# Smaller TensorE tiles for the query repeats and the key sums, another order of the first loads, and a new plan, in a fused sketched-attention and feed-forward kernel

## The chip, the cores and the metric

The kernel runs on one core of a Trainium2 chip. The metric is the device time of one execution in microseconds (us): the median of three runs. A profile of one further execution says how the time is spent. The engines are named as the profile names them: PE is TensorE's matmuls and PEld its weight loads, DVE is VectorE, ACT is ScalarE, POOL is GpSimd, and SP is the engine that mostly issues DMAs. A "q" behind an engine's name (SPq, ACTq) is its instruction queue, where DMAs are issued.

## The reference

Four batches of four heads, 1088 tokens each, 32 numbers a head. Queries and keys are sketched: two products with 8x32 matrices, then the outer product of the two, 64 features. Attention is then a sum over keys, with no softmax; its output goes through a feed-forward layer with a squared relu.

```python
def phi(x):                                   # 64 features of a token
    a = np.einsum('rd,bhsd->bhsr', S1, x)
    b = np.einsum('rd,bhsd->bhsr', S2, x)
    return np.einsum('bhsi,bhsj->bhsij', a, b).reshape(*x.shape[:-1], r * r)
q_p, k_p = (phi(q), phi(k))
kv = np.einsum('bhsf,bhsd->bhfd', k_p, v)     # key sums
z = np.sum(k_p, axis=2)
num = np.einsum('bhsf,bhfd->bhsd', q_p, kv)   # read-out
den = np.einsum('bhsf,bhf->bhs', q_p, z)[..., None] + 1e-06
attn = (num / den).astype(np.float32)
x = attn.transpose(0, 2, 1, 3).reshape(4352, 128)
r = np.maximum(x @ w_in, 0.0)                 # 128 -> 2048
out = ((r * r) @ w_out).astype(np.float32)    # 2048 -> 128
```

Attention is computed in float32, the feed-forward layer in bfloat16.

## The kernel before

**The plan.** The kernel is written as a graph of operations. Each has a cost on one or more engines, operations that it depends on, buffers that it takes, and a priority worked out from a due time. Ahead of the launch a list scheduler (`Graph.run`) walks through the graph with these costs and sorts the operations by their planned start. Each engine then executes its own instructions strictly in that order, and real waits come from semaphores. So an operation that is planned early but is late on the chip holds back what is queued behind it on its engine.

**Buffers.** PSUM holds three h buffers of two banks (128 x 1024 float32), one o buffer (the feed-forward output) and one a buffer. Tensors of a batch (kin, kT, qin, qT, vin, vp, ka, kp, kvz, qp) exist twice, by batch parity.

**Attention of a batch**, by the lines of the profile:
- Loads of k, q and v on SP's queue (L297, L333, and L340 for the last 64 tokens of v, which go to a tile of their own, vtl). For batch 0, k and q come in two parts, and the first values go on ScalarE's queue.
- VectorE transposes keys in 32x32 blocks (L365). Key sketches (L379): per chunk of 32 tokens a column tile of 32, 128 rows, S1 and S2 side by side. ScalarE copies the S1 half (L387), VectorE multiplies both into kp, 64 features a head (L395).
- Values are copied into vp beside a column of ones (L350, L353), on GpSimd, or for batch 0 on ScalarE.
- Key sums (L412): for each of nine steps of 128 tokens and each head, weights are 64 features of kp, and the 33 columns of vp are moved; heads go alternately to the two 64-column halves. The sum is copied to the state kvz in two copies (L425), each head's 64 features on the partition half where its sketch of the query will be, the rest zero.
- VectorE transposes queries (L434). Query repeats (L447): S1 repeated along one index of the 64 features and S2 along the other, by one product each. A product takes a pair of heads (64 rows of qT) and gives 128 rows, two heads of 64 features; the two pairs stand in two banks of an h buffer. There are three groups of up to 384 columns, and an h buffer each for S1 and S2.
- ScalarE copies the S1 buffer (L456), VectorE multiplies (L460) into qp.
- Read-out (L477): per chunk of 32 tokens a column tile of 32, weights qp, moved the state of a head pair, 66 columns. VectorE divides (L487 to L489), TensorE transposes (L500), and ScalarE or VectorE copies to xT (L506), the feed-forward input.

**Feed-forward** works in nine blocks of tokens (384, seven times 512, 384) and eight steps of 256 hidden units: two products (L527) into an h buffer, relu on ScalarE (L536), square on VectorE (L543), two accumulating products into o (L550). A block ends with a transpose by VectorE (L557) and four or eight stores (L566).

**The weights** come through six loads on GpSimd's queue (L275, L279), behind a one-column copy that reads the last key column (`gate`, L271), so that they start when batch 0's keys are there.

In numbers of the trace, a float32 product stands as two records of weights and two of matmul (two passes).

Of the kernel before, what the change touches and what calls it, by code (L numbers as in the profile page):

```python
# [15 lines left out]
SEM = 0.07  # L16
LOOK = 0.12
DMA_FIRST = 1.05
DMA_LAST = 1.2
# [9 lines left out]
class Op:  # L29
    def __init__(self, name, alts, fn, deps, pri, alloc, uses, port, dma, after):  # L30
        self.name, self.alts, self.fn, self.pri = name, alts, fn, pri
        self.deps = [d for d in deps if d is not None]
        self.alloc, self.uses, self.port, self.dma = alloc, uses, port, dma
        self.after = [d for d in after if d is not None]
        self.look = LOOK
        self.start = self.end = self.eng = None


class Graph:

    def __init__(self, slots):
        self.ops = []
        self.slots = {k: [[0.0, None] for _ in range(n)] for k, n in slots.items()}

    def add(self, name, alts, fn, deps=(), pri=0.0, alloc=(), uses=(), port=(), dma=None, after=()):
        op = Op(name, alts, fn, deps, pri, list(alloc), list(alloc) + list(uses), port, dma, after)
        for b in op.uses:
            b.pending += 1
        self.ops.append(op)
        return op  # L50

    def slot_time(self, buf):
        best = None
        for kind in buf.kinds:
            for i, (t, b) in enumerate(self.slots[kind]):
                if b is not None and b.pending:
                    continue
                if best is None or t < best[0] - 0.3:
                    best = (t, (kind, i))
        return best  # L60

    def run(self):
        eng_free, port_free, pipe = {}, 0.0, 0.0
# [8 lines left out]
        while ready:  # L72
            cands = []
            for o in ready:
                t_slot = 0.0
                ok = True
                for b in o.alloc:
                    s = self.slot_time(b)
                    if s is None:
                        ok = False  # L80
                        break
                    t_slot = max(t_slot, s[0] + SEM)
                if not ok:
                    continue
                best = None
                for e, (busy, lat, *pen) in o.alts.items():
                    pen = pen[0] if pen else 0.0
                    t = max(eng_free.get(e, 0.0), t_slot)
                    for d in o.deps:
                        t = max(t, d.end + (SEM if d.eng != e else 0.0))  # L90
                    for d in o.after:
                        t = max(t, d.start)
                    if e in o.port:
                        t = max(t, port_free)
                    if o.dma is not None and e != "POOL" and len(lanes) >= 8:
                        t = max(t, lanes[-8])
                    if best is None or t + lat + pen < best[0]:
                        best = (t + lat + pen, t, e, busy, lat)
                cands.append((best[1], o, best))
            assert cands, "no operation can start: " + ", ".join(o.name for o in ready[:20])  # L100
            t0 = min(c[0] for c in cands)
            _, o, (_, t, e, busy, lat) = min(
                (c for c in cands if c[0] <= t0 + c[1].look), key=lambda c: (c[1].pri, c[0]))
            for b in o.alloc:
                b.slot = self.slot_time(b)[1]
                self.slots[b.slot[0]][b.slot[1]] = [t, b]
            o.start, o.end, o.eng = t, t + lat, e
# [5 lines left out]
            eng_free[e] = t + busy  # L113
            if e in o.port:
# [16 lines left out]
def act(n):  # L131
    return (0.833e-3 * n + 0.17, 0.833e-3 * n + 0.2)


def dve(n, rate=1.042e-3, fix=0.07):
    return (rate * n + fix, rate * n + fix + 0.04)


def pool(n, rate=2.4e-3):
    return (rate * n + 0.12, rate * n + 0.16)  # L140


def pe(t):
    return (t, t + 0.2)


@with_exitstack
def kernel(
    ctx: ExitStack,
    tc: tile.TileContext,  # L150
    q: bass.AP,
    k: bass.AP,
    v: bass.AP,
    S1: bass.AP,
    S2: bass.AP,
    moe_w_in: bass.AP,
    moe_w_out: bass.AP,
    out: bass.AP,
):
    nc = tc.nc  # L160
    B, H, S, D = q.shape
    R = S1.shape[0]
    F = R * R
    d_ff = moe_w_in.shape[1]
# [5 lines left out]
    assert (B, H, D, R, S) == (4, 4, 32, 8, 1088)  # L170

    sb = ctx.enter_context(tc.tile_pool(name="sb", bufs=1))
    ps = ctx.enter_context(tc.tile_pool(name="ps", bufs=1, space=bass.MemoryType.PSUM))

    def T(name, shape, dt=F32):
        return sb.tile(shape, dt, name=name, tag=name)

    def P(name, shape, dt=F32):
        return ps.tile(shape, dt, name=name, tag=name)

    NH, NA, NR, NB = 3, 1, 4, 2
    G = Graph({"h": NH, "o": 1, "a": NA, "r": NR, "g": NR, "osb": 3, "den": 3, "A": 2})
# [8 lines left out]
        "A": [T(f"A{i}", [128, 2, 384]) for i in range(2)],  # L191
# [7 lines left out]
    ident = T("ident", [128, 128], BF16)  # L199
    S_sb = T("S_sb", [128, 32])  # L200
    ST = T("ST", [128, 32])
    mk4 = T("mk4", [128, H])
    mk2 = T("mk2", [128, 2])
    SK = T("SK", [128, 2, H, R])
    SR = T("SR", [128, 2, 2, R, R])
# [8 lines left out]
    vtl = [T(f"vtl{i}", [32, H, 2, D]) for i in range(NB)]  # L214
# [3 lines left out]
    kvz = [T(f"kvz{i}", [128, 2, 2, D + 1]) for i in range(NB)]  # L218
# [5 lines left out]
    for x, src in ((0, S1), (1, S2)):  # L224
        def f(e, x=x, src=src):
            en = nc.sync if e == "SP" else nc.scalar
            en.dma_start(out=S_sb[x::2, :], in_=src[None, :, :].to_broadcast([8, R, D]))  # L227
        SU[x] = add(f"S{x}", {"SP" if x else "ACT": (0.4, 2.0)}, f, pri=-200, dma=0.05)
    o_mkz = add("mkz", {"DVE": dve(4)}, lambda e: nc.vector.memset(mk4, 0.0), pri=-100)

    def f_mk(e):
        for h in range(H):
            nc.vector.memset(mk4[32 * h : 32 * h + 32, h : h + 1], 1.0)
        nc.vector.tensor_tensor(out=mk2, in0=mk4[:, 0:2], in1=mk4[:, 2:4], op=ALU.add)
    o_mk = add("mk", {"DVE": (0.4, 0.45)}, f_mk, [o_mkz], pri=-100)
    o_ST = add("ST", {"DVE": dve(32)}, lambda e: nc.vector.transpose(ST, S_sb), SU, -98)
    STx = ST[:, 0 : 2 * R].rearrange("p (r x) -> p x r", x=2)

    o_SR = []
    for x in range(2):  # L240
        def f(e, x=x):
            s = STx[:, x]
            s = s[:, None, None, :] if x else s[:, None, :, None]
            nc.vector.tensor_tensor(
                out=SR[:, x], in0=s.to_broadcast([128, 2, R, R]),
                in1=mk2[:, :, None, None].to_broadcast([128, 2, R, R]), op=ALU.mult)
        o_SR.append(add(f"SR{x}", {"DVE": dve(128)}, f, [o_ST, o_mk], -96))

    def f_SK(e):
        nc.vector.tensor_tensor(  # L250
            out=SK, in0=STx[:, :, None, :].to_broadcast([128, 2, H, R]),
            in1=mk4[:, None, :, None].to_broadcast([128, 2, H, R]), op=ALU.mult)
    o_SK = add("SK", {"DVE": dve(64)}, f_SK, [o_ST, o_mk], -97)

    z_ops = {}
    for i in range(NB):
# [4 lines left out]
        z_ops[i] = add(f"z{i}", {"POOL": (0.6, 0.7)}, f_z, pri=-100 + i)  # L261
# [3 lines left out]
        ident, iot, 0, op=ALU.is_equal), [o_iota], -60)  # L265

    wo_src = moe_w_out.rearrange("(G c e) d -> c G (e d)", c=128, e=E)
    wo_dst = w_out.rearrange("c (G e) d -> c G (e d)", e=E)
    o_win, o_wout = [], []
    gate = T("gate", [128, 1])  # L270
    o_gate = add("gate", {"POOL": (0.1, 0.15)}, lambda e: nc.gpsimd.tensor_copy(gate, kin[0][:, S - 1 : S]), [], -45)  # L271
    gated = [o_gate]
    for lo, hi in ((0, 1), (1, 2), (2, 4)):
        def f(e, lo=lo, hi=hi):
            nc.gpsimd.dma_start(out=w_in[:, 512 * lo : 512 * hi], in_=moe_w_in[:, 512 * lo : 512 * hi])  # L275
        o_win.append(add(f"w_in{lo}", {"POOL": (0.9, 3.0)}, f, [z_ops[1]] + gated, -40 + lo, dma=0.8 * (hi - lo)))
# [3 lines left out]
        o_wout.append(add(f"w_out{lo}", {"POOL": (1.0, 3.0)}, f, [z_ops[1]] + gated, -39.5 + lo, dma=0.9 * (hi - lo)))  # L280
# [10 lines left out]
    def attention(b, vt):  # L291
        i = b % NB
        mine = lambda key, op: hist.setdefault((b, key), []).append(op)

# [7 lines left out]
        def tok(j, g):  # L302
            if j == 8:
# [326 lines left out]
```

## Time and profile before

| | us |
|---|---|
| median of 3 runs (132.34, 134.12, 134.55) | 134.12 |
| span of the profiled execution (first to last instruction) | 130.5 |
| PE busy | 115.0 |
| DVE busy | 96.6 |
| ACT busy | 81.6 |
| POOL busy | 11.1 |
| mean granted clock of TensorE | 0.979 of full |

The profiled execution's span lies inside its time; what lies around it is the difference to the runs, 3.6 us against the median. Busy times of engines overlap, and a PE that is busy is not PE at its peak, since the ends of its pipelined matmuls are modelled. The page cuts the span into 40 slices of 3.26 us and gives each engine's busy share of a slice in tenths. The chain of waits follows the last instruction back, each time to what released it, so its pieces add up to the span.

### The profile page before, as it was taken

How to read it: one execution, taken by the hardware profiler on the slowest of the kernel's cores; microseconds unless marked ns; L12 is line 12 of the kernel's file. 1: busy time of each engine (PE TensorE's matmuls, PEld its weight loads, DVE VectorE, ACT ScalarE, POOL GpSimd, SP SyncE). 2: the span in 40 equal slices, each digit the busy share in tenths (PEclk: the TensorE clock that was granted, in tenths of full speed). 3: DMA queues.
4: the chain of work that ended last, by engine and by line, in shares of the span. 5: the costliest groups of instructions: out<-in, count | busy, mean ns of one | idle time of the engine just before them, and what ended most of it. 6: DMA issues, size and time to landing. Idle time of an engine off the chain costs nothing.

```text
span 130.5 us, 3742 instructions
## 1 busy us (share of the span) xinstructions
PE 115.0 (88%) x1572; PEld 62.2 (48%) x1572; DVE 96.6 (74%) x170; ACT 81.6 (63%) x108; POOL 11.1 (9%) x30
## 2 busy tenths in 40 slices
PE   0279599599999899999999999999999999999930
PEld 0256365353565455455445655556355544444500
DVE  2486367969969999969837888798268977878840
ACT  0065023377636749986525979885377699999910
POOL 4091000504250000000000000000000000000000
PEclk9999959999999999999999999999999999999996
DMA  1999999996700210220130001301300040031402
GB/s 21 296 135 242 328 254 260 254 225 223 159 3 0 51 17 0 40 45 0 28 58 0 5 0 28 57 0 25 60 0 5 0 80 5 3 65 18 78 16 50
DMA packets 24225, 10.22 MB, mean 78 GB/s; under 512 B 19472, under 2 KB 22928, under 8 KB 24208
## 3 DMA queue, kind: packets, MB, share of 16 engines
q1 hardware_dynamic: 22280, 8.57, 28.1%
q0 software_dynamic: 992, 1.05, 5.3%
q10 hardware_dynamic: 936, 0.37, 1.3%
q8 instruction: 12, 0.20, 0.6%
q14 instruction: 5, 0.04, 0.1%
HBM read 8.80 MB, written 2.23 MB: 85 GB/s over the span
## 4 chain that ended last, share of the span: by engine, by line
PE 70%; DMA 9%; DVE 7%; ACT 6%; issue 2%; ACTq 2%; DVEq 0%
PE o L550 21%; PE h L527 18%; PE h L447 14%; ACT r L536 6%; PE a L412 5%; DMA qin<-in_q_dram 5%; PE a L477 4%; DMA vin<-in_v_dram 4%; PE h L477 3%; DVE g L543 3%; PE a L379 2%; DVE osb L557 2%; PE h L500 1%; PE h L379 1%; ACTq L227 1%
## 5 line engine op out<-in xcount | busy, mean ns | idle before, releaser
L536 ACT ACTIVATE r<-h 128x1024 bf16<-128x1024 f32 (+1 forms) x72 | 65.6, 1026 | 19.7 <-PE h L527 19.5
L543 DVE TENSOR_TENSOR g<-r 128x1024 bf16<-128x1024 bf16 (+1 forms) x72 | 46.8, 662 | 11.3 <-ACT r L536 10.7
L550 PE MATMUL o<-g,w_out 128*128 128x512 bf16 (+1 forms) x144 | 40.9, 368 | 0.7 <-DVE g L543 0.4
L527 PE MATMUL h<-xT,w_in 128*128 128x512 bf16 (+1 forms) x144 | 40.1, 369 | 0.7 <-ACT r L536 0.4
L447 PE MATMUL h<-qT,SR 64*128 64x384 f32 (+1 forms) x96 | 22.3, 560 | 1.3 <-DVE qT L434 1.3
L527 PEld LDWEIGHTS <-w_in 128*128 128x128 bf16 x144 | 15.1, 114 | 15.7 <-issue 4.5
L550 PEld LDWEIGHTS <-w_out 128*128 128x128 bf16 x144 | 12.1, 97 | 15.8 <-issue 6.9
L460 DVE TENSOR_TENSOR qp<-h,A 128x768 f32<-128x768 f32 (+1 forms) x12 | 10.9, 907 | 5.7 <-PE h L447 5.1
L456 ACT COPY A<-h 128x768 f32<-128x768 f32 (+1 forms) x12 | 9.2, 763 | 7.5 <-PE h L447 7.5
L447 PEld LDWEIGHTS h<-qT,SR 64*128 64x128 f32 x96 | 8.3, 202 | 9.0 <-issue 4.3
L412 PEld LDWEIGHTS a<-vp,kp 128*64 128x64 f32 x288 | 9.3, 143 | 3.7 <-issue 3.7
L412 PE MATMUL a<-vp,kp 128*64 128x33 f32 x288 | 10.1, 228 | 0.0
L379 PE MATMUL a<-SK,kT 128*32 128x64 f32 x168 | 3.8, 239 | 5.6 <-DVE kT L365 5.6
L365 DVE STREAM_TRANSPOSE kT<-kin 128x1088 f32<-128x1088 f32 (+2 forms) x5 | 5.4, 1073 | 3.0 <-DMA kin<-in_k_dram 3.0
L434 DVE STREAM_TRANSPOSE qT<-qin 128x384 f32<-128x384 f32 (+1 forms) x8 | 5.9, 734 | 2.0 <-DMA qin<-in_q_dram 1.9
L557 DVE STREAM_TRANSPOSE osb<-o 128x512 f32<-128x512 f32 (+1 forms) x9 | 6.1, 682 | 1.0 <-PE o L550 0.8
L395 DVE TENSOR_TENSOR kp<-a,ka 128x1024 f32<-128x1024 f32 (+1 forms) x5 | 6.4, 1272 | 0.6 <-ACT ka L387 0.6
L477 PEld LDWEIGHTS h<-kvz,qp 128*32 128x32 f32 x288 | 5.0, 120 | 3.1 <-issue 1.5
L379 PEld LDWEIGHTS a<-SK,kT 128*32 128x32 f32 x168 | 2.9, 121 | 7.1 <-DVE kT L365 5.6
L350 POOL COPY vp<-vin 128x512 f32<-128x512 f32 x6 | 4.1, 706 | 22.9 <-DMA vin<-in_v_dram 16.2
L477 PE MATMUL h<-kvz,qp 128*32 128x66 f32 x288 | 6.1, 238 | 0.0
L477 PEld LDWEIGHTS a<-kvz,qp 128*32 128x32 f32 x288 | 4.4, 109 | 2.5 <-issue 1.3
(42 smaller groups left out, 55.0 us busy)
## 6 DMA issues: line engine op xcount, KB each, us to landing
kin<-in_k_dram SPq DMA_DIRECT2D x3, 544.0 KB, 8.4
qin<-in_q_dram SPq DMA_DIRECT2D x3, 544.0 KB, 8.2
vin<-in_v_dram SPq DMA_DIRECT2D x12, 128.0 KB, 8.3
out_dram<-osb SPq DMA_DIRECT2D x16, 64.0 KB, 1.9
out_dram<-osb SPq DMA_DIRECT2D x8, 48.0 KB, 2.2
qin<-in_q_dram SPq DMA_DIRECT2D x1, 352.0 KB, 6.6
vin<-in_v_dram ACTq DMA_DIRECT2D x5, 64.0 KB, 4.1
out_dram<-osb SPq DMA_DIRECT2D x8, 40.0 KB, 1.7
```

The lines of the kernel that those rows point to most:

```text
L379: nc.tensor.matmul(o[32 * g : 32 * g + 32, :, j - j0, :], lt, SK.rearrange("p x h r -> p x (h r)"), start=True, stop=True)
L395: nc.vector.tensor_tensor(out=kp[i][:, j0:j1].rearrange("p j h (x y) -> p (j h) x y", y=R), in0=bb[:, :, None, :].to_broadcast([128, m, R, ...
L412: nc.tensor.matmul(t[64 * (h % 2) : 64 * (h % 2) + 64, 33 * (h // 2) : 33 * (h // 2) + 33], kp[i][:, j, h, :], vp[i][:, h, j, :], start=(j ...
L447: nc.tensor.matmul(at(hb)[:, 512 * pr : 512 * pr + n], SR[64 * pr : 64 * pr + 64, x].rearrange("p a x y -> p (a x y)"), qT[i][64 * pr : 64 ...
L456: nc.scalar.copy(at(sA)[:, :, 0:n], at(hA).rearrange("p (m s) -> p m s", m=2)[:, :, 0:n])
L460: nc.vector.tensor_tensor(out=qp[i][:, :, c0 : c0 + n], in0=at(hB).rearrange("p (m s) -> p m s", m=2)[:, :, 0:n], in1=at(sA)[:, :, 0:n], o ...
L477: nc.tensor.matmul(t[32 * cc : 32 * cc + 32, x, 2 * pr : 2 * pr + 2, :], qp[i][:, pr, 32 * c : 32 * c + 32], kvz[i][:, pr], start=True, st ...
L527: nc.tensor.matmul(at(hb)[:, step * w : step * w + N], w_in[:, 512 * (ct // E) : 512 * (ct // E) + 512].rearrange("p (c e) -> p e c", e=E) ...
L536: nc.scalar.activation(o, view(at(hb)), ACTF.Relu)
L543: nc.vector.tensor_tensor(out=at(gb)[:, 0 : W * N], in0=r, in1=r, op=ALU.mult)
L550: nc.tensor.matmul(at(ob)[:, 0:N], w_out[:, ct, :], at(gb)[:, N * w : N * w + N], start=(ct == 0), stop=(ct == CT - 1))
L557: nc.vector.transpose(at(sbuf)[:, 0:N], at(ob)[:, 0:N])
```

## The change

- **Query repeats**: instead of two products with a pair of heads each (64 rows, 128 columns), one call makes sixteen products a group, one for each of two sketches, two halves of the columns (`w`) and four heads: 32 rows, 64 columns of the array, 192 (160) columns moved. In the second half of the columns the two heads of a pair swap partition halves, so that all eight 32x64 tiles are used. S1 and S2 of a head pair now share one h buffer, S1 first, and copy and multiplication are done per pair: two of half the size for each of before.
- **Swapped state**: kvz has a second version with the heads on the other halves, made by two more copies; the read-out takes the version that belongs to its chunk.
- **Key sums**: each head's 64 features are split in two products with 32 weight columns, on four 32-column tiles.
- **First loads**: both S loads and the first four value loads (six of the eight steps) are issued on ScalarE's queue, everything else on SP's. The first key load has 24 of 34 chunks instead of 16. The tail of the values goes straight into vp with two loads. The copy that gates the weight loads reads the first values instead of the last keys. All value copies are on GpSimd.
- **TensorE at the start**: sixteen matmuls of 512 columns on a tile of zeros, at the lowest priority.
- **The plan**: per-engine waiting times, a price for changing the tile mode, new costs, and tables of priorities per operation and batch (STEP, SHIFT, SPAN). Relu is always on ScalarE, and six squares out of 72 go to ScalarE (SQ_ACT).

The core of the diff:

```diff
+SIZES = (384, 512, 512, 512, 512, 512, 512, 512, 384)
+SQ_ACT = {
+    (0, 5), (3, 0), (3, 3), (3, 4), (4, 3), (5, 4),
+}
+WARM = 16
...
+    warm = None
+    for n in range(WARM):
+        def f(e):
+            nc.tensor.matmul(tiles["o"][0], wz[:, 0:128], wz, start=True, stop=True)
+        warm = add(f"warm{n}", {"PE": pe(0.43 if n < 8 else 0.216)}, f, [o_wz, warm], 400, mode="full")
...
-    o_gate = add("gate", {"POOL": (0.1, 0.15)}, lambda e: nc.gpsimd.tensor_copy(gate, kin[0][:, S - 1 : S]), [], -45)
+    o_gate = add("gate", {"POOL": (0.1, 0.15)}, lambda e: nc.gpsimd.tensor_copy(gate, vin[0][:, 0, 0, 0:1]), [], -70)
...
-        KS = ((0, 16), (16, 34)) if b == 0 else ((0, 34),)
+        KS = ((0, 24), (24, 34)) if first else ((0, 34),)
...
+                o_v[a].append(add(f"ldv{b}.{a}{g}", {"ACT" if first and not a else "SP": (0.45, 3.4)}, f, prev(b, "vp") + after,
+                                  pri("ldv") + 0.1 * a, dma=0.5 * (j1 - j0) / 8))
...
+            en.dma_start(out=vp[i][0:32, :, 8, 0:D], in_=vsrc[:, :, 32, :])
+            en.dma_start(out=vp[i][32:64, :, 8, 0:D], in_=vsrc[:, :, 33, :])
...
-                    for h in range(H):
-                        nc.tensor.matmul(
-                            t[64 * (h % 2) : 64 * (h % 2) + 64, 33 * (h // 2) : 33 * (h // 2) + 33],
-                            kp[i][:, j, h, :], vp[i][:, h, j, :],
-                            start=(j == 0 and h < 2), stop=(j == NJ - 1), skip_group_check=True)
+                    for hh in range(2):
+                        for hp in range(2):
+                            h = 2 * hh + hp
+                            for u in range(2):
+                                p0 = 64 * hp + 32 * u
+                                nc.tensor.matmul(
+                                    t[p0 : p0 + 32, 33 * hh : 33 * hh + 33],
+                                    kp[i][:, j, h, 32 * u : 32 * u + 32], vp[i][:, h, j, :],
+                                    start=(j == 0 and hh == 0), stop=(j == NJ - 1), skip_group_check=True)
...
+        for w in range(2):
+            for hp in range(2):
...
+                    d = 64 * (hp ^ w)
+                    fn(kvz[i][d : d + 64, w, :, hp, :],
+                       at(kvb)[64 * hp : 64 * hp + 64, 0:66].rearrange("p (m d) -> p m d", m=2))
...
+            c0, N = 384 * g, 192 if g < 2 else 160
+            hs = [Buf("h"), Buf("h")]
+
+            def f_qr(e, hs=hs, c0=c0, N=N):
+                for x in range(2):
+                    for w in range(2):
+                        for h in range(H):
+                            p0 = 64 * ((h % 2) ^ w)
+                            nc.tensor.matmul(
+                                at(hs[h // 2])[p0 : p0 + 64, 512 * w + N * x : 512 * w + N * x + N],
+                                SR[32 * h : 32 * h + 32, x].rearrange("p x y -> p (x y)"),
+                                qT[i][32 * h : 32 * h + 32, c0 + N * w : c0 + N * w + N], start=True, stop=True)
```

## The prediction

> **What bounds the kernel now.** I read the 40 slices of the page first, then the stretches between visible changes of pace, then the chain of waits in order of time, then the timeline of the start. The slices (busy tenths):
>
> ```profile
> PE   0279599599999899999999999999999999999930
> DVE  2486367969969999969837888798268977878840
> ACT  0065023377636749986525979885377699999910
> ```
>
> TensorE is full from slice 9 to slice 37, but not for the first eight slices (26 us). Then the stretches (start:end, length, busy us of each engine, granted clock, DMA share, GB/s):
>
> ```profile
> 15.00:20.00 5.00, 4.56 (x60) 2.51 (x60) 3.04 (x7) 1.01 (x2) 0.00 (x0) 0.66 1.12 269
> 26.30:103.50 77.20, 76.74 (x1117) 40.71 (x1117) 62.20 (x108) 53.18 (x68) 4.31 (x8) 1.00 0.20 43
> 103.50:125.50 22.00, 21.26 (x102) 10.22 (x100) 17.79 (x29) 20.78 (x25) 0.00 (x0) 1.00 0.22 38
> ```
>
> In the 77.2 us of the middle TensorE is busy for 76.74, VectorE for 62.2 (81%), ScalarE for 53.2 (69%): what comes off TensorE there comes off the time, until VectorE or ScalarE is as full. After 103.5 only feed-forward work is left, and ScalarE (20.8 of 22.0) is level with TensorE. The chain prices batch 2's share of the middle (start, us, what):
>
> ```profile
> 59.49 0.84 PE h L447 x4
> 60.34 1.06 PE a L412 x32
> 61.39 0.54 PE o L550 x2
> ...
> 64.72 1.29 PE a L412 x40
> ...
> 66.54 0.85 PE h L447 x4
> ...
> 67.94 0.74 PE h L447 x4
> 68.68 0.83 PE a L477 x48
> ```
>
> L447 is the query repeats (six entries a batch), L412 the key sums (two), L477 the read-out (three); key sketches (L379) are 0.58 and 0.70. Feed-forward pairs take 0.43, or 0.54 just behind attention work. Last, the start, where TensorE's order costs time:
>
> ```profile
> 11.42 2.67 PE L412 MATMUL a<-vp,kp 128*64 128x33 f32 x72
> 15.44 1.43 PE L447 MATMUL h<-qT,SR 64*128 64x384 f32 x4 [1.35 <-DVE qT L434]
> 16.80 1.55 PE L477 MATMUL h<-kvz,qp 128*32 128x66 f32 x48
> 20.65 0.34 PE L500 MATMUL h<-ident,xs 128*128 128x128 bf16 x3
> 22.55 0.51 PE L527 MATMUL h<-xT,w_in 128*128 128x384 bf16 x2
> ```
>
> The first feed-forward matmul starts at 22.55. The read-out at 16.80 stood behind a repeat that waited for the second query load (issued 7.84, landed 14.47), and both ran under a clock of 0.66.
>
> **TensorE work now**, from warm rows: feed-forward 112 pairs x 0.43 + 32 x 0.33 = 58.7 (pairs counted over both products); key sketches 4 x 1.28 = 5.1; key sums 4 x 2.34 = 9.4; repeats 4 x (4 x 0.84 + 2 x 0.74) = 19.4; read-out 12 x 0.83 = 10.0; transposes 12 x 0.2 = 2.4; 0.11 behind each of some 40 attention entries = 4.4. Sum 109.4. By 26.3 some 13 is done (batch 0: 1.28 + 2.34 + 4.84 + 2.5 + 0.4 of transposes; 0.58 of batch 1; three pairs of 0.33), so 96.4 is left, and takes 99.2 to 125.5: 97% use. The last transpose, its store and the end take 5.0. That gives the span of 130.5; the median of the runs, 134.12 (132.34 to 134.55), has 3.6 more around it, which I keep.
>
> **Query repeats.** A group of 384 columns now takes two entries (S1 and S2), each two 64-row tiles side by side: 0.84 + 0.84. Of this, two passes of 0.32 stream and 0.19 is entry: back to back, eight records take 1.49 in the chain, so an entry of four costs about 0.65 once running. The change makes one entry of 16 products of 192 columns on eight 32x64 tiles, half of the columns on each column half. Two products per tile, each half as long as now: 2 x 0.32 + 0.19 = 0.83 if all eight run together. So 0.84 for 384, 0.74 for 320 columns: 2.42 a batch against 4.84, 2.4 saved. No row has 32x64 tiles. The bounds: all eight together (L447 shows two row tiles together, L379 four column tiles: 40 records of 0.25 mean, 9.9 in sum, end within 0.70), or only four, which streams 1.29 + 0.19 and saves 0.2 a group. I take eight, because both kinds of concurrency stand in rows.
>
> [...]
>
> **Key sums.** 72 records a batch become 144, with weights of 32 columns instead of 64. In the chain 32 take 1.06 and 40 take 1.29: 0.030 a record and 0.09 an entry. Key sketches (four tiles, 32-column weights, 64 columns moved) have (0.70 - 0.58)/8 = 0.015. Bounds: 0.015 again, because 32-column weights set it (144 x 0.015 + 0.18 = 2.34: nothing gained), or half, 0.0075, since four tiles run where two did and columns moved are 33, not 64 (1.26). [...]
>
> The L379 rows have 40 loads of 0.12 and 40 matmuls of 0.25 within 0.70, so loads and matmuls of column tiles overlap. [...]
>
> **Other engines.** Six squares leave VectorE (5 x 0.685 + 0.58 = -4.0) for ScalarE (+6, by the relu rows of 1.055 and 0.92). Products and copies of the repeats halve in size and double in number: 12 more of each, at a fixed cost read from L460 (0.950 at 768, 0.820 at 640: 0.17) and L456 (0.15): +2.0 and +1.8. Eight more state copies of 0.21: +0.8 each. Batch 0's value copies (1.8) go from ScalarE to GpSimd, where 768 columns cost about 1.06 by 0.706 for 512. VectorE 96.6 becomes 95, ScalarE 81.6 becomes 89. Both hide under TensorE, but the middle shrinks by 3 x 3.4 to 67, and there each has about 61 (VectorE 62.2 - 3.4 + 2.1, ScalarE 53.2 + 5.3 + 2.0), 90% instead of 81% and 69%. Relu stays where it is: all 72 are on ScalarE now.
>
> TensorE, 109.4 - 9.7 - 4.0, comes to 95.8.
>
> **The start.** Four value loads and both S loads go to ScalarE's queue, 384 of 544 KB of keys come first, and the weights wait for the first value loads instead of the keys (gate at 6.53 now; values landed at 7.8). They stand ahead of all ScalarE work as six issues did before (to 5.15), so nothing is added there. The tail of the values becomes two loads on SP's queue instead of one, 0.4 each, in a queue that mostly waits for results to store (70.6 us on osb), and saves GpSimd two copies of 0.34. Behind the gate stand GpSimd's six weight loads: first w_in now issued at 6.65, landed 5.7 later; even 2 us late it lands at 14.4, before it is needed. TensorE gets 16 matmuls of 512 columns on zeros ahead of the keys; 16 x 0.22 to 0.43 = 3.5 to 7 us, and TensorE is idle to 5.59 now, so 0 to 1.5 us of delay; I take nothing, since the key load covers them. What they could give is the warm price: the first key sketches take 1.08 instead of 0.58, the first two repeats 2.93 instead of 1.49.
> From the rows the first feed-forward can come earlier by: key sums and read-out at full price 1.3 + 0.65; waits in TensorE's order (state ready at 15.73, read-out 16.80; scaled rows at 19.44, transpose 20.65; xT at 21.50, matmul 22.55) 3.3. That is 22.55 - 5.2 = 17.3. Bounds: 22.5 if the new order puts as much in between, 14 if keys and values also come 3 us earlier.
>
> **Sum.** At 17.3 sketches, sums, one repeat and one read-out of batch 0 are done (1.28 + 1.33 + 0.84 + 0.83 = 4.3). Left: 91.5. Use falls from 97% to 95%, because two more engines stand at 90%: 96.3. Then 17.3 + 96.3 + 5.0 = 118.6 in the span, 122.2 with what lies around it: 122.
>
> **Rivals.** (1) The other engines or the order take the gain: the product groups hold two of three h buffers at once, and VectorE at 95 needs its own order. With use at 88% and the first feed-forward at 20: 20 + 104 + 5 + 3.6 = 132.6; at 91%, 129. For it: VectorE stands at 9 in 10 of the 24 slices of the middle already. Against: between 26 and 103 the chain is TensorE but for one relu of 1.03.
> (2) The start gives nothing (22.5): 122.2 + 5.2 = 127.4.
> (3) Half of the tiles run together: 12 groups x 0.65 = 7.8 more: 130.
> (4) Slower: the array starts products in strict order, a product's second pass holds back those behind it, and the 32 passes of a group run two deep: 32 x 0.163/2 + 0.19 = 2.8 a group, 23 us over the sum: 145. It decides from about three deep (1.9 a group), where the other gains are eaten up. Four-deep L379 rows speak against it; that 32x64 tiles mix row and column tiles is all that speaks for it.
> (5) The change doesn't do what it says on keys: no gain per record, +4: 126.
>
> **Numbers.** The forecast with (2) and (5), which lie within it: 0.68; (1) 0.14, (3) 0.08, (4) 0.10. The forecast's own range is 114 (first matmul at 14, 98% use: 116; entries at nothing, 12 x 0.19: 2.3 less) to 128. The overall range is 114 to 133: it leaves out (4) and some of (1). Runs differ by 2.2 us of 134, so 2% is about what a measurement can tell. Faster by 2% means under 131.4: all of the forecast, two thirds of (1), over half of (3): 0.81. Within 2%: 0.08. Slower: 0.11.
>
> **What would show it.** L447's successor with mean entries near 0.84 in the chain and 12 entries, not 24 (2.8 would be rival 4, 1.5 rival 3); key sums of 1.3 a batch with 576 records; first w_in matmul near 17; clock 1.00 before 20 us; TensorE over 90% busy in the middle. If TensorE has holes there that end on r, g or qp, rival 1 holds.

## The result, and the profile after

| | before | after |
|---|---|---|
| median of runs, us | 133.23 (132.28 to 134.55, 4 runs) | 127.91 (127.34 to 128.89, 4 runs) |
| ratio, 95% interval | 1 | 0.9618 [0.9515, 0.972] |
| span of the profiled run, us | 130.46 | 125.56 |
| TensorE matmuls and weight loads (records) | 1,572 of each | 2,164 of each |

The kernel is faster by 3.8%, about 5.3 us. The forecast was 122, with a span of 118.6; the span is 125.56. The direction was right and the range held the time, but more than half of the forecast gain is missing; in the span it is 7.0 us. Some executions of a kernel are in a slower state; the ratios, here and below, compare the fast runs of both kernels, made side by side, while the medians take in all runs.

The 40 slices of the changed kernel, with TensorE's granted clock, its chain by engine and the queue that loads TensorE's instructions:

```profile
PE   6974937879947999998599999999999999999930
DVE  2369362569974999999759989499777997978840
ACT  0062210759837767689299999988788799999910
PEclk9999595899999999999999999999999999999999
PE 75%; issue 8%; DMA 6%; DVE 3%; ACTq 2%; SPq 1%; POOL 1%; ACT 0%; DVEq 0%
q8 instruction: 17, 0.28, 1.0%
```

A slice is 3.14 us. TensorE has dents at 16, 35 and 60 us (the 3 or 4 of slices 6 and 12, the 5 of slice 20), the last two where it was full before. "issue", time in which the engine waited for nothing that the profile shows, was 2% of the chain and is 8%. The last line will matter: 17 instruction loads on queue q8, where before there were 12. The stretches (start:end, length, busy us of PE, PEld, DVE, ACT and POOL, granted clock, DMA share, GB/s):

```profile
15.00:20.00 5.00, 2.15 (x86) 1.53 (x74) 1.89 (x5) 0.87 (x2) 0.00 (x0) 0.84 1.21 230
26.30:98.00 71.70, 67.18 (x1534) 37.76 (x1532) 61.62 (x117) 58.35 (x83) 2.61 (x4) 1.00 0.21 46
98.00:120.50 22.50, 21.62 (x149) 11.14 (x149) 19.13 (x34) 20.87 (x25) 0.00 (x0) 1.00 0.21 37
```

In the middle TensorE is idle for 4.5 us of 71.7 (0.5 of 77.2 before). VectorE and ScalarE stand at 86% and 81% there, so neither of them is the bound. From 15 to 20 us TensorE works for 2.15 of 5. The chain in order of time shows where the idle time lies (start, us, what; L463 is the key sums, L501 the repeats, L541 the read-out, L591 the first feed-forward product):

```profile
13.86 1.57 PE h L501 x32
...
16.57 0.31 PE a L541 x5
16.88 2.68 issue
19.56 1.53 PE a L541 x43
...
23.23 0.88 PE h L591 x4
24.11 0.81 PE a L541 x43
24.92 0.83 issue
...
34.95 0.94 PE a L463 x66
35.90 2.19 issue
...
41.62 0.84 PE h L501 x32
...
57.89 1.34 PE a L463 x115
59.23 1.82 issue
...
76.62 0.69 PE a L463 x59
81.57 0.88 PE a L463 x71
```

Four times TensorE stops in the middle of an entry (one row of the chain, the matmuls of one operation) whose inputs and buffers are all there: 2.68 + 0.83 + 2.19 + 1.82 = 7.5 us. Away from the stops the new shapes run as they should: a repeat entry takes 0.84, and a batch's key sums take 0.69 + 0.88.

The stops have something in common that no view prints but that can be counted in the trace. Every matmul and every weight load is a record of TensorE; numbered from the start, the records behind which it stops are 699, 955, 1,464 and 2,486. They lie 256, 509 and 1,022 apart. Between them stand 0, 3 and 2 instructions of TensorE that wait for semaphores; with these the distances are 256, 512 and 1,024, which is one, two and four times 256. And at each stop a load of 16,384 bytes on queue q8 is under way, or, at record 955, has ended 0.49 us before (us from the span's start; the numbers are read from the trace's records):

```
stop      record   load starts  load ends   TensorE goes on
16.88        699         16.83      18.08             19.56
24.92        955         23.48      24.43             25.75
35.90      1,464         35.48      36.55             38.08
59.23      2,486         58.57      59.86             61.05
```

TensorE goes on 1.2 to 1.5 us after the load has ended, 2.3 to 2.7 us after it started. 17 loads of 256 make 4,352, near the kernel's 4,328 records; before, 12 loads made 3,072, near its 3,144. At the other block ends TensorE went on without such a stop. From these counts and distances I take it that a load of 16,384 bytes brings 256 instructions.

### The profile page after: what moved, and what is told of

The parts are those of the page before. It is cut to its first block, busy times and chain, and to the rows that moved or that the text cites. A ratio compares the mean times of both kernels' runs of the same rounds, so it can differ in the third digit from the quotient of the medians.

```text
span 125.6 us, 4949 instructions
## 1 busy us (share of the span) xinstructions
PE 107.6 (86%) x2164; PEld 60.3 (48%) x2164; DVE 93.9 (75%) x184; ACT 86.0 (68%) x122; POOL 10.3 (8%) x26
## 4 chain that ended last, share of the span: by engine, by line
PE 75%; issue 8%; DMA 6%; DVE 3%; ACTq 2%; SPq 1%; POOL 1%; ACT 0%; DVEq 0%
PE o L618 25%; PE h L591 24%; PE h L501 8%; PE a L541 6%; PE a L463 5%; DMA S_sb<-in_S_dram 4%; DMA qin<-in_q_dram 2%; PE h L541 2%; PE h L425 2%; DVE osb L625 2%; PE a L425 1%; PE a L564 1%; ACTq L272 1%; PE h L564 1%; ACTq L700 1%
## 5 line engine op out<-in xcount | busy, mean ns | idle before, releaser
L591 PE MATMUL h<-xT,w_in 128*128 128x512 bf16 (+1 forms) x144 | 39.7, 369 | 0.3 <-DVE xT L570 0.3
L591 PEld LDWEIGHTS <-w_in 128*128 128x128 bf16 x144 | 15.5, 114 | 13.3 <-issue 1.3
L516 ACT COPY A<-h 128x384 f32<-128x384 f32 (+1 forms) x24 | 9.9, 464 | 9.6 <-PE h L501 9.4
L463 PE MATMUL a<-vp,kp 128*32 128x33 f32 x576 | 7.3, 203 | 6.3 <-issue 4.0
L521 DVE TENSOR_TENSOR qp<-h,A 128x384 f32<-128x384 f32 (+1 forms) x24 | 11.6, 526 | 1.3 <-ACT A L516 1.2
L501 PE MATMUL h<-qT,SR 32*64 32x192 f32 (+1 forms) x384 | 11.7, 356 | 0.0
L541 PE MATMUL a<-kvz,qp 128*32 128x66 f32 x384 | 8.5, 233 | 3.7 <-issue 3.5
L463 PEld LDWEIGHTS a<-vp,kp 128*32 128x32 f32 x576 | 6.3, 113 | 9.3 <-issue 6.5
L541 PEld LDWEIGHTS a<-kvz,qp 128*32 128x32 f32 x384 | 6.7, 116 | 6.9 <-issue 6.2
L501 PEld LDWEIGHTS h<-qT,SR 32*64 32x64 f32 x384 | 7.2, 145 | 2.9 <-issue 1.4
L304 PE MATMUL o<-wz 128*128 128x512 bf16 x16 | 5.9, 541 | 1.2 <-DVE mk L276 1.2
L609 ACT ACTIVATE g<-r 128x1024 bf16<-128x1024 bf16 (+1 forms) x6 | 6.1, 1022 | 0.7 <-PE o L618 0.5
L442 DVE TENSOR_TENSOR kp<-a,ka 128x1024 f32<-128x1024 f32 (+2 forms) x4 | 5.6, 1410 | 0.8 <-ACT ka L434 0.8
```

The lines of the kernel that those rows point to most:

```text
L304: nc.tensor.matmul(tiles["o"][0], wz[:, 0:128], wz, start=True, stop=True)
L463: nc.tensor.matmul(t[p0 : p0 + 32, 33 * hh : 33 * hh + 33], kp[i][:, j, h, 32 * u : 32 * u + 32], vp[i][:, h, j, :], start=(j == 0 and hh ...
L501: nc.tensor.matmul(at(hs[h // 2])[p0 : p0 + 64, 512 * w + N * x : 512 * w + N * x + N], SR[32 * h : 32 * h + 32, x].rearrange("p x y -> p ...
L516: nc.scalar.copy(at(sA)[:, :, 0:N], view(m, 0))
L521: nc.vector.tensor_tensor(out=qp[i][:, m, c0 : c0 + 2 * N].rearrange("p (w s) -> p w s", w=2), in0=view(m, 1), in1=at(sA)[:, :, 0:N], op=A ...
L541: nc.tensor.matmul(t[32 * cc : 32 * cc + 32, x, 2 * pr : 2 * pr + 2, :], qp[i][:, pr, 32 * c : 32 * c + 32], kvz[i][:, w, pr], start=True, ...
```

## The experiments

The theory, F in the expectations: TensorE runs out of instructions. A float32 product is four records in these traces (two matmuls and two weight loads), the change multiplies the products by making the tiles smaller, and where they are executed faster than the next block comes, the engine stands still at a block's end. The rival, H: the stop belongs to the operation, by a wait that the profile doesn't show (the 32x64 tiles, or the read-out behind them). A further theory, D, is about the early stop: the data loads, which fill the DMA engines then (share 1.21 from 15 to 20 us), hold the instruction loads up.

**More records ahead of the stop.** Each matmul on zeros was split into six, or into two, of fewer columns, everything else staying as it was:

```diff
-            nc.tensor.matmul(tiles["o"][0], wz[:, 0:128], wz, start=True, stop=True)
+            for i in range(6):
+                nc.tensor.matmul(tiles["o"][0][:, 0 : 512 // 6], wz[:, 0:128], wz[:, 0 : 512 // 6], start=True, stop=True)
```

> Each of the 16 matmuls on zeros becomes six of 85 columns: 160 more TensorE records (weight loads and matmuls) ahead of all work, the columns streamed stay the same, and so does every engine's order. The changed kernel's four long TensorE pauses that wait for nothing (2.68, 0.83, 2.19 and 1.82 us, 7.5 in all) come 256 records or multiples of it apart (records 699, 955, 1464, 2486 in the trace), each with a 16 KB instruction load in flight. Theory F: TensorE runs out of instructions at the ends of 256-record blocks when the records just before such an end are short. Then the pauses move by 160 records to other operations; by the changed kernel's own record times most ends then fall behind feed-forward work, and the pauses should add up to 0 to 3 us: 121 to 125 us. Rival H: the pauses belong to the operations in which they stand (tile shapes, PSUM): they stay in the same L541 and L463 entries, and the time stays at 127 to 129.

> Each of the 16 matmuls on zeros becomes two of 256 columns: 32 more records ahead of all work. Theory F: block ends move by 32 records, within or near the same dense entries, so pauses add up to 4 to 9 us again, but stand elsewhere: 125 to 129 us. Rival H: the same pauses in the same entries, 127 to 129.

With six the time was 126.09 (125.14 to 126.66), ratio 0.961 [0.9515, 0.9705]. The timeline of TensorE in this kernel (start, us, line, tiles, count, idle before):

```profile
13.43 0.90 PE L502 MATMUL h<-qT,SR 32*64 32x192 f32 x5
18.48 1.57 PE L502 MATMUL h<-qT,SR 32*64 32x192 f32 x27 [4.14 <-issue]
```

The first stop has moved out of the read-out into the repeats (L502 is L501 of the changed kernel, one line on), and it is behind record 699 again. The second is behind 955 again. At 1,463 TensorE is idle for 0.27, but the chain has VectorE in front of it, which makes the sketched keys (kp), and the block's load had ended 2.7 us before; at 2,486 there is no gap. That is what F says and H cannot: the place is a record number, not an operation. The time is above the 121 to 125 expected, as the early stop grew to 4.14. With two the time was 128.18 (127.21 to 129.01): stops behind 699 again (4.45) and 1,462 (3.20).

**Fewer records: key sums on 64 columns again**, the repeats left on 32x64 tiles (72 products a batch become 36):

```diff
-                            for u in range(2):
-                                p0 = 64 * hp + 32 * u
-                                nc.tensor.matmul(
-                                    t[p0 : p0 + 32, 33 * hh : 33 * hh + 33],
-                                    kp[i][:, j, h, 32 * u : 32 * u + 32], vp[i][:, h, j, :],
+                            nc.tensor.matmul(
+                                t[64 * hp : 64 * hp + 64, 33 * hh : 33 * hh + 33],
+                                kp[i][:, j, h, :], vp[i][:, h, j, :],
```

> Only the key sums go back to weights of 64 columns (two column tiles), with the plan unchanged: 576 of 4328 records fewer, each batch's key sums at 2.1 to 2.3 us instead of some 1.6. Theory F: about 3 us more streaming against fewer and slower-read blocks; pauses of 0 to 4 us instead of 7.5: 123 to 130 us, and pauses at other operations. Rival H (pauses belong to 32x64 and four-tile entries): pauses at L463 vanish (4.0 us), those at L541 stay: 126 to 128.

123.92 (122.6 to 125.12), ratio 0.9397 [0.9242, 0.9552]: 4.0 below the change in the median, with key sums that stream 3.1 us longer (4 times 2.35 against 1.57). The two were not run side by side; their ratios to the kernel before are 2.2% apart, and the intervals overlap by a little. Its chain:

```profile
17.55 3.28 issue
20.83 0.63 PE h L499 x3
```

The early stop is there, in the third repeat now, behind record 698 (one record is missing from this trace). It is the only one: from 22 to 115 us no gap between TensorE's records is over 0.24 us. The chain has later pieces of 0.68, 0.99 and 0.79 called "issue", but they stand between instructions of ScalarE.

**Fewer records the other way: repeats on 64 rows again**, two row tiles of 128 columns, key sums left on 32 columns (the sketch weights SR, made for two heads at once, and the read-out, which takes the unswapped state throughout, are changed to match):

```diff
-                        for h in range(H):
-                            p0 = 64 * ((h % 2) ^ w)
+                        for m in range(2):
...
-                                at(hs[h // 2])[p0 : p0 + 64, 512 * w + N * x : 512 * w + N * x + N],
-                                SR[32 * h : 32 * h + 32, x].rearrange("p x y -> p (x y)"),
+                                at(hs[m])[:, 512 * w + N * x : 512 * w + N * x + N],
+                                SR[64 * m : 64 * m + 64, x].rearrange("p a x y -> p (a x y)"),
```

> Only the repeats go back to products of 64 rows and 128 columns (two row tiles instead of eight 32x64 tiles); plan, buffers, copies and multiplications stay, and the read-out takes the unswapped state throughout. Streaming per entry 1.28 instead of 0.64 for 384 columns; by the prediction's sum 12 x 0.6 = 7.4 us more on TensorE, if nothing else: 134 to 136. By theory F 384 records fewer and slower-read blocks give some of it back: pauses of 2 to 5 us instead of 7.5, and 129 to 133.

127.33 (126.98 to 130.79), ratio 0.9575 [0.949, 0.966]. Its chain has one stop and repeats as slow as before the change:

```profile
16.72 2.47 issue
...
37.76 1.50 PE h L504 x16
```

Repeats of 1.50 and 1.29 instead of 0.84 and 0.73 are 8 x 0.66 + 4 x 0.56 = 7.5 us more streaming, and the time is no longer than the change's. It is also under the 129 to 133 that F had expected. The stops are 2.5 instead of 7.5 us, which gives back 5.0, and between 6 and 120 us there is one stretch at a granted clock of 0.50 (3.4 us) instead of two; how much that gives was not measured.

**Both tile changes undone**, with the new plan, loads and zeros kept:

> Both tile changes undone (repeats of 64 rows, key sums of 64 columns), everything else of the change kept: what the new plan and first loads bring alone, with 3400 records, close to the kernel before (3144). By streaming alone, 7.9 us more for the repeats than the kernel with 64-column key sums only (123.9): 130 to 132. Theory F: with this few records no block end costs over 1 us after 26 us, so less than that is lost: 125 to 129.

126.62 (125.73 to 128.12), ratio 0.9543 [0.9372, 0.9713]; the first feed-forward product starts at 20.00. The slices:

```profile
PE   6985888999999999999999999999999999999930
```

No dent is left behind the first 12.5 us: from 19 to 117 us TensorE is never idle for more than 0.28 us, at the end of a block (record 698) for 0.25, and the granted clock is 0.997 over the run. So the plan and the loads alone give as much as the whole change. The four combinations, medians in us, measured at different times beside the kernel before at 133.2 to 133.9:

| | repeats on 64 rows | repeats on 32x64 tiles |
|---|---|---|
| key sums on 64 columns | 126.6 | 123.9 |
| key sums on 32 columns | 127.3 | 127.9 |

The repeats' change takes 7.5 us off the streaming, the key sums' 3.1. The first brings 2.7 us beside 64-column key sums, and nothing beside the others; the second costs 0.7 or 4.0, of which only the 4.0 is clear of the scatter of the single runs.

**Records without a change of tiles.** That fewer records help could still be a matter of the tiles. So in the kernel with the old tiles each read-out product of 66 columns was split into two of 33 with the same weights; 1,152 records are added:

```diff
+                        for d in range(2):
...
-                            nc.tensor.matmul(
-                                t[32 * cc : 32 * cc + 32, x, 2 * pr : 2 * pr + 2, :],
-                                qp[i][:, pr, 32 * c : 32 * c + 32],
-                                kvz[i][:, 0, pr], start=True, stop=True)
+                                nc.tensor.matmul(
+                                    t[32 * cc : 32 * cc + 32, x, 2 * pr + d, :],
+                                    qp[i][:, pr, 32 * c : 32 * c + 32],
+                                    kvz[i][:, 0, pr, d], start=True, stop=True)
```

> Old tile shapes throughout (126.6, 3348 records, no pause over 0.8 us), but each read-out product of 66 columns becomes two of 33 with the same weights: 1152 records more, the same columns streamed, no new tile shape. Theory F (records per time, whatever the tile): pauses of 3 to 8 us at record numbers 699, 955, 1460 or 256 and its multiples from there, 129 to 134. Rival H (the new tile shapes cause the pauses): no pauses, at most 1 to 2 us for loads that no longer hide: 126.6 to 128.6.

136.19 (134.12 to 137.28), ratio 1.0326 [0.9907, 1.0746], 9.6 above the kernel with the old tiles (ratio 0.9543 [0.9372, 0.9713]) and above the 129 to 134 that F had expected. A read-out entry takes 0.96 instead of 0.83, which is 12 x 0.13 = 1.6. The chain shows the most of the rest:

```profile
16.85 4.47 issue
...
27.06 1.56 issue
...
73.69 1.56 issue
```

Where the kernel with the old tiles had one stop of 0.25 us, there are 7.6 us in these three, behind records 698, 954 and 2,986, with an instruction load under way in each. No tile of the array has changed, only the columns moved. F is shown, and H falls.

**The early stop and the data loads.** Batch 2's loads, or those of batches 1 and 2, were held until a division of batch 0, with this and a move of the loads in the order:

```diff
+                if b == 0 and g == 2:
+                    nc.vector.memset(kin[2 % NB][:, 0:1], 0.0)
```

> Batch 2's loads (1.6 MB, in the changed kernel issued from 14.0 to 21 us while the DMA engines are full) are held on SP's queue until batch 0's last division, by a one-column memset on the tile that they overwrite; no other order changes. Theory F with D (an instruction load takes its turn among the data loads, so that block ends before 26 us cost most): the pauses at records 699 and 955 (2.68 and 0.83 us) shrink to 1 to 2 us in all, weights and batch 1 land earlier, and the time falls by 1 to 3 us, to 125 to 127; the pause at 1464 may move or grow, since the held loads then run until about 35 us. Rival: an instruction load takes what it takes whatever the data loads do: 127 to 129.

> Batch 1's loads too are held, until batch 0's first division (16.8 us), batch 2's as before; tiles as in the changed kernel. If data loads delay instruction loads (theory D): with only the weights in flight the pause at record 699 falls from 2.7 to 3.3 us to 1.5 or less, and the time to 125 to 127; what batch 1 then lacks may cost 1 us near 30 us. Rival: instruction loads are as slow without data loads: pause 2.5 or more, 127 to 130.

Batch 2's alone gave nothing: 128.55 (127.67 to 131.51), with an early stop of 3.31. With batch 1's as well the load that ends the early stop starts at 14.59 instead of 16.83, the stop shrinks from 2.68 to 1.34, and the first feed-forward product comes at 19.2 instead of 23.23. So D fits the early stop here, in one profiled execution. It is not shown as a rule: with 64-column key sums, both batches held and a new order (the last row of the table further down) that load started at 18.11, where it started at 18.28 with nothing held, and the stop was 2.66. And the time is 127.53 (125.98 to 129.64), within the scatter of the change's 127.91, as a later stop grew:

```profile
32.10 4.53 issue
```

It is behind record 1,460, in key sums, and after it the granted clock is 0.50 from 34.5 to 41.3. The gain was given back at a later block.

**The zeros.** The 16 matmuls move 4 columns instead of 512, so that TensorE does next to nothing before the sketches (0.53 us instead of 5.32); the records stay:

```diff
-            nc.tensor.matmul(tiles["o"][0], wz[:, 0:128], wz, start=True, stop=True)
+            nc.tensor.matmul(tiles["o"][0][:, 0:4], wz[:, 0:128], wz[:, 0:4], start=True, stop=True)
```

> The 16 matmuls on zeros move 4 columns instead of 512: as many records, so block ends stay where they are, but TensorE is idle at the start. If the matmuls earn their place by the clock: first key sketches of some 32 ns a record instead of 18, and 0.5 to 2 us more in all (128.5 to 130). The prediction's term for them was nothing: 127 to 129, because the first key sums wait for copied values till 11.5 us in either case.

130.62 (129.06 to 132.23), ratio 0.9792 [0.9672, 0.9912]: 2.7 us above the change in the median. The first 48 sketch records take 1.51 without the long zeros, 0.88 with them. But the four stops add up to 10.6 us here instead of 7.5, so how much of the 2.7 comes of the slower sketches stays open.

**The S loads.** The second S load, which lands at 6.5 behind 544 KB of keys, was put first on SP's queue:

```diff
-            nc.scalar.dma_start(out=S_sb[x::2, :], in_=src[None, :, :].to_broadcast([8, R, D]))
+            if x:
+                return
+            nc.scalar.dma_start(out=S_sb[0::2, :], in_=S1[None, :, :].to_broadcast([8, R, D]))
+            nc.sync.dma_start(out=S_sb[1::2, :], in_=S2[None, :, :].to_broadcast([8, R, D]))
```

> The second S load goes first on SP's queue, ahead of the keys, as in the kernel before. In the changed kernel S lands at 6.5 us, behind 544 KB of keys, and the first key sketches wait for it till 7.15 with keys transposed at 4.83. If this late start is on the path: sketches at about 5.6 to 6.0 and 1 to 1.5 us off the time (126 to 127). If not, because the first key sums wait for values that GpSimd copies until 11.5: no change (127 to 129).

A miss: 133.29 (130.78 to 137.58, 10 runs), ratio 1.0001 [0.994, 1.0061]. The keys landed later in turn, and the sketches start at 7.12 as before (7.15). The stops add up to 10.2 instead of 7.5, with two more stretches at a granted clock of 0.50. Why they are longer was not tried.

**Towards a better kernel**, from the one with 64-column key sums: batch 2's loads held, those of batches 1 and 2 held, and each with the value copy ahead of the weights' issues and batch 0's first transposes ahead of its last repeat.

> The held loads of batch 2 together with key sums of 64 columns (alone 123.9 us, with one pause of 3.28 us at record 698, from 17.5 us on). By theory F with D that pause falls to about 1 us and the time to 121 to 123; by the rival it stays at 123.9.

> The same with key sums of 64 columns (123.8 with batch 2 held alone, pause of 2.1 us at record 698). Theory D: pause under 1 us, 121 to 123. Rival: 2 us or more, 123.5 to 125.

> As 64-column key sums with batch 2 held (123.8), and two steps in another order: GpSimd copies the first values before it issues the first weight load (0.68 us earlier), and batch 0's first transpose goes ahead of its third repeat on TensorE. If the start is on the path, the first key sums come 0.6 us and the first feed-forward matmul 1 to 2.5 us earlier than 21.2: 121.5 to 123. If the instruction load at record 698 sets it, no change: 123.3 to 124.5.

> 64-column key sums, batches 1 and 2 held, first value copy and first transpose earlier: the three edits that each left the time at 123.2 to 123.8, together. If what is left at the start is the instruction load at record 698 (0.84 us with both batches held): 121.5 to 123. If the edits only move the pause: 123 to 124.

| | median, us | ratio to before |
|---|---|---|
| 64-column key sums | 123.92 | 0.9397 [0.9242, 0.9552] |
| and batch 2 held | 123.81 | 0.9217 [0.9086, 0.9348] |
| and batches 1 and 2 held | 123.16 | no interval |
| batch 2 held, new order | 123.34 | 0.9331 [0.9246, 0.9415] |
| batches 1 and 2 held, new order | 124.19 | 0.949 [0.9286, 0.9693] |

The five medians lie within 1.1 us and can't be told apart, and none of the four additions reached the lower of its expected ranges (121 or 121.5 to 123). All five are faster than both kernels, by some 4 us than the change. In each profiled execution a single stop of more than half a us is left at a block's end: 3.28, 2.10, 0.84, 1.82 and 2.66 in the order of the table.

## Why the prediction was wrong

**The step that failed is the sum**: "Use falls from 97% to 95%, because two more engines stand at 90%", and the 17.3 in front of it. Both took it that TensorE, its inputs being there, has its next instruction; no term stands for the stops, and idle time was looked for at the other engines and in TensorE's order alone. The runs showed 7.5 us of stops at block ends in its place, 2.68 ahead of the first feed-forward product at 23.23 and 4.84 behind it. Where the prediction adds 17.3 + 96.3 + 5.0, the profiled run has 23.23 + 97.3 + 5.0: of the 7.0 us that are missing in the span, 5.9 are in the start and 1.0 behind it. Behind it, the sum made again from the trace: from 23.23 to 120.5 are 97.3 us; of the work that the prediction had left, 91.5, two repeats and a read-out (2.4) were done earlier than it assumed, and key sums are 0.7 more: 89.8. Over 97.3 - 4.84 = 92.4 that is 97% use, better than the 95% forecast. So the 4.84 us of stops were set off, all but 1.0, by 1.7 less of work and by that better use. That this part of the sum came within 1.0 us is luck.

The records tell where it was to be seen, from rows that the prediction had. Records are the matmuls and weight loads of an entry, and the rate is theirs over its duration:

| entry | records in us | a block of 256 lasts, us |
|---|---|---|
| feed-forward pair | 4 in 0.43 | 27 |
| repeat, before | 8 in 0.84 | 27 |
| repeat, 32x64 tiles | 64 in 0.84 | 3.4 |
| key sums of a batch, 64 columns | 144 in 2.34 | 4.2 |
| key sums of a batch, 32 columns | 288 in 1.57 | 1.4 |
| read-out | 96 in 0.83 | 2.2 |

At the four stops TensorE went on 2.3 to 2.7 us after the load's start. The change brings two of its entries near or under that. Before it only the read-out was under it, in entries shorter than a block with slower records around them.

**The start: 23.23 instead of 17.3.** Rival 2 (the start gives nothing, 22.5) is what happened to the first feed-forward product. The timeline of the changed kernel:

```profile
11.57 1.11 PE L463 MATMUL a<-vp,kp 128*32 128x33 f32 x96 [1.84 <-POOL vp L401]
17.36 0.56 DVE L553 TENSOR_TENSOR xs<-h,rec 128x384 bf16<-128x384 f32 x1
22.32 0.46 PE L564 MATMUL h<-ident,xs 128*128 128x128 bf16 x3
23.23 0.88 PE L591 MATMUL h<-xT,w_in 128*128 128x384 bf16 x4 [0.28 <-DVE xT L570]
```

Of the 5.9 us, 2.68 are the early stop. TensorE's order costs too, as the prediction's bound of 22.5 had it ("if the new order puts as much in between"): the scaled rows xs are ready at 17.92, but their transposes (L564) stand behind the second read-out, in which the stop falls, and the third repeat, until 22.32. The granted clock was 0.50 from 12.4 to 15.8 and from 19.2 to 22.6, and entries there took up to nearly twice as long (a repeat 1.57 instead of 0.84). The key sums begin at 11.57, 1.84 after TensorE fell idle, for the value copy that now stands on GpSimd behind its gate and weight issues; "Behind the gate stand GpSimd's six weight loads" costed the loads and not this copy. "Clock 1.00 before 20 us" was right only from 5.5 to 12.4 and from 15.8 to 19.2. How the 3.3 us beside the stop divide among these was not tried.

**The zeros** were taken at nothing, and the shorter entries that they could give were counted for the key sums and the read-out only. Without them the kernel took 2.7 us more, with 3.1 us more of stops.

**The repeats were right**: 0.84 and 0.73 for an entry of 16 products, where 0.84 and 0.74 were forecast for all eight tiles together, and rivals 3 (1.5) and 4 (2.8) are refuted by the chain. Heads 0 and 1 write the same columns of one h buffer, on different partition halves, and the entry takes 0.84 all the same. The streaming was saved as forecast (4.84 a batch became 2.41); of the time, 2.7 us arrived beside 64-column key sums.

**The key sums were mis-sized**: 1.57 a batch for 1.33, from 2.34. 36 products became 72 and took two thirds of the time, so rival 5, by which nothing was to be gained per record, is refuted as to streaming. No run shows the 1.33, nor the 4.0 of four batches that the sum takes off with it: the runs showed 1.57 and 3.1, and a weight load that went from 143 ns with 64 columns (L412, before) to 113 ns with 32 (L463). As to time nothing was gained, for a cause that the prediction had not named.

**The other engines were right**: VectorE 93.9 and ScalarE 86.0, forecast 95 and 89, both hidden. Rival 1 had the right place, idle time on TensorE in the middle, and the wrong cause: "holes there that end on r, g or qp" are not what is there; the stops end on nothing that the profile shows.

**The rest of the time.** 3.6 us were added around the span; the profiled run of the changed kernel has 127.34 - 125.56 = 1.8, and that of the kernel before 132.28 - 130.46 = 1.8. The 3.6 came of setting a span against the median of other executions, which lie 2.2 us apart.

## What to carry to other kernels

Where a change cuts products into smaller tiles, count TensorE's records per microsecond besides the streaming time: a float32 product here was four of them, and where 256 of them lasted less than some 3 us, the engine stopped at the block's end (in the changed kernel 2.2 us up to 35.90, 1.4 up to 59.23); at the start, while the data loads ran, longer blocks were too short as well (3.8 up to 16.88, 5.4 up to 24.92). The 3 us are an estimate from the stop at 59.23, where the load started 0.7 after TensorE had begun the block ahead, and TensorE went on 2.5 after that; in the kernel with split read-outs two blocks of 3.0 and 3.1 us (51.1 to 57.2) passed without a stop. In these profiles a stop showed as "issue" of TensorE in the middle of an entry, at instruction numbers a multiple of 256 apart, with a load on the instruction queue under way or, once, ended 0.49 us before. Of two tile changes try first the one that saves more time per record that it adds: here the repeats (7.5 us of streaming for 384 records beside the same plan), not the key sums (3.1 for 576).

## What the runs showed of the hardware

- An instruction load takes 0.9 to 1.4 us in the changed kernel, but at the four stops TensorE goes on only 1.2 to 1.5 us after its end. The loads follow TensorE closely: with its semaphore instructions counted, each of the loads from 46 to 98 us started between 0.3 us before and 1.2 us after TensorE began, or after a stop went on with, a block of 256. I take it that each brought the next block, so that no more than one was ahead. Earlier, with a DMA share of 1.21 from 15 to 20 us and 1.11 from 20 to 26.3, the loads came later: the load that starts at 16.83 came 3.8 us after its block had begun at 13.0, that at 23.48 came 3.9 after TensorE went on at 19.56. That the data loads cause this is likely, but not shown.
- Some stops were followed by a granted clock of 0.50, in the middle of the kernel too: with the zeros split in two, a stop of 3.20 at 35.68 and the clock at 0.50 from 37.9 to 44.7, where feed-forward pairs took 0.85 instead of 0.43; with batches 1 and 2 held, 4.53 at 32.10 and 0.50 from 34.5 to 41.3. Stops of 2.46 with the narrow zeros (at 37.34) and 1.97 with batch 2 held (at 61.03) were each followed by 3.4 us at 0.50, those of 2.19 and 1.82 in the changed kernel by none. So such a stop can cost more than its length.
